# Copies of q and k through DRAM spread over two issuing queues from the first unit on, and four-term x sums at fixed places on VectorE

## The chip, the core and the metric

The kernel runs on one NeuronCore of a Trainium2 chip. The core has a matrix engine (TensorE, PE in the profile), a vector engine (VectorE, DVE), a scalar engine (ScalarE, ACT), GpSimd (POOL) and a synchronising engine (SyncE, SP) that here does little but issue DMAs. Each engine runs its own instructions in order and waits on semaphores for the others. ScalarE too can issue DMAs; such an issue then stands in ScalarE's own instruction order, among its evictions. The page writes ACTq and SPq for what these engines' queues do beside computing. The metric is device time in microseconds.

## The reference, cut to what matters

```python
# lightning attention: q, k, v of (B 4, H 8, S 768, D 64), a decay lam for each head, blocks of 64
for b in range(nb):
    intra = einsum(einsum(qb, kb) * Dmask, vb)
    inter = einsum(qb * lam_pow, kv_state)
    out[:, :, sl] = intra + inter
    kv_state = lam_block * kv_state + einsum(kb * rev_pow, vb)
# bridge: (B,H,S,D) -> x of (3072, 512); then four experts
p = domain_probs / (domain_probs.sum(-1, keepdims=True) + 1e-09)
for e in range(4):
    h = maximum(x @ w1[e], 0)          # w1[e]: 512 x 1024
    out += p[:, e:e + 1] * (h @ w2[e]) # w2[e]: 1024 x 512
```

All of it is fp32.

## The kernel before

The 3072 tokens are cut into three groups of 1024. A **unit** is one expert on one group; there are twelve, in the order group 0 with experts 0, 1, 2, 3, group 1 with 1, 2, 3, 0, group 2 with 2, 3, 0, 1. Both products of an expert are done in Strassen's way: seven products M1 to M7 of half-size blocks in place of eight, each of sums of blocks of the weights and of x. Most of these seven are cut once more in the same manner. The sums of weights are made by GpSimd ahead of time, written to DRAM (`w_ops`, `w_sums`) and read again (`ws_in`, `w2t`); the sums of x (tile `xs`, one "slot tile" for each of the seven) are made in place, by GpSimd for group 1 and by VectorE for the second unit and for group 2.

**Opening part.** The first chunks of attention run mixed with the first product of the first unit, `direct_product` (L1482, matmuls at L1503), in the order `SEQ0` = M1, M2, M5, M6, M7, M3, M4; the loop for the last five is at L1617 to 1632. Each of these has four quarters, and `sums_then` names what else is put behind a quarter.

**Main loop** (L1661 to 1755). For each unit there are seven steps, and each step has eight slots x = 0 to 7. In the slots the second product of the unit at hand (`second_product` L1086, matmuls into banks `q` at L1101, gate-weighted accumulation on VectorE at L1115 and L1119) alternates with the first product of the next unit (`first_product` L1023, matmuls into banks `pg` at L1047, in the order `SEQ` = M1, M5, M6, M2, M7, M3, M4). A `pg` bank is emptied by a copy on ScalarE at L1055 where its target is fresh, else by an addition on VectorE (helper `tt`, L117), followed for some targets by a relu on ScalarE at L1059. There are two `pg` banks in turn. From the sixth unit on both products are cut twice.

**The order is written out by hand** (`manual_schedule`): every engine executes in the order in which the Python code calls it. A planner on the Python side decides when some of the calls come: `now` counts slots, `busy` estimates GpSimd's backlog, `moved` that of the DMA engines (`send`, L109), `asked` that of SyncE (each `send` without a named engine adds 0.27 slots), `filled` that of VectorE. `pump` (L202) is called in each slot and takes the next chore (preparing weights on GpSimd) when GpSimd is free and neither `moved` nor `asked` is too far ahead. `until` forces chores that are needed now. `take(own_sums)` lets VectorE do one waiting x sum.

**DMAs.** `send` issues on SyncE unless an engine is named. DMAs issued on SyncE and on ScalarE share a ring of completion semaphores, so that an issue on the one can wait for an earlier DMA of the other. SyncE issues the loads of the weights (`w1b`, `w2b`), the stores of their sums, and the loads that feed the products: `feed` (L945) for `ws_in`, `feed2` (L1071) for `w2t`.

**Copies through DRAM.** The last two of six chunks of the sequence (`SECOND` = 4 on) get q and k by way of a DRAM tile `across`, in which the rows lie as the attention of group 2 wants them. `bring_across` (L453) lists 128 pieces, for q and k, 4 × 4 blocks and 4 batches; a piece copies 32 KB from DRAM to DRAM in runs of 128 B. All name `nc.scalar` as the issuing engine. `trickle` (L463) issues the next piece. It is called once per quarter in the last two products of the opening part, then in each odd slot of the main loop, and from step 4 on in slot 4 as well. `load_more` (L481), when the first chunk of a batch b is to be loaded, first issues all pieces of batches up to b that are left, and then loads `qx` and `kx` from `across` (`load_across`).

**Sums of x for the second unit.** `own(m)` (L1471) is a chore for each m: it has GpSimd make the weight operands for product m of the second unit, lets `own_x(m)` (L1433) append four in-place x subtractions to `own_sums`, and marks the product as fed. Subtractions not taken from `own_sums` by the time that `first_product` starts product m are all issued there, in a block.

Of the kernel before, what the change touches and what calls it, by code (L numbers as in the profile page):

```python
# [21 lines left out]
def kernel(  # L22
# [30 lines left out]
    nc = tc.nc  # L53
# [55 lines left out]
    def send(out, in_, by=None):  # L109
        n = 4 * min(packet(out), packet(in_))  # L110
        moved[0] = max(moved[0], now[0]) + 4 * math.prod(out.shape) / n * (9 + n / 25) / 16 / 1714
        if by is None:
            asked[0] = max(asked[0], now[0]) + 0.27
        (by or nc.sync).dma_start(out=out, in_=in_)
# [336 lines left out]
    pieces = []  # L451

    def bring_across(b):  # L453
        for x, of in enumerate((q, k)):
            for y in range(4):
                for ac in range(NHP):
                    src = of[b, 4 * (y // 2) + ac, SECOND * C:, (y % 2) * 32:(y % 2 + 1) * 32]
                    to = across[x, y * 32:(y + 1) * 32, ac, b]
                    pieces.append((b, lambda to=to, src=src: send(
                        out=to, in_=src.rearrange("(t p) d -> p t d", p=32), by=nc.scalar,  # L460
                    )))

    def trickle(m=1):  # L463
        for _ in range(m):
            if pieces:
                pieces.pop(0)[1]()

    def comes_across(n):
        return where(n)[0] >= SECOND
# [472 lines left out]
    SEQ = ("M1", "M5", "M6", "M2", "M7", "M3", "M4")  # L942
# [490 lines left out]
    def own_x(m, g=0, wait=0):  # L1433

        steps = to_do[m] = []

        def sub(f):
            def step():
                steps.pop()
                f()  # L1440
                if not steps:
                    made.add(("x", g, m))

            steps.append(step)

        for f in x_steps(g, m, nc.vector):
            sub(f)
        own_sums.extend(after(wait, f) for f in steps)
# [22 lines left out]
    def own(m):  # L1471
        if m not in own_ops:
            own_weights(m)
        own_x(m)
        fed[0, 1, m] = own_ops[m]


# [56 lines left out]
    def x_sums(*halves):  # L1534

        all_added()

        for name, a, b in (("T1", "B12", "B11"), ("T2", "B22", "T1"), ("T3", "B22", "B12"), ("T4", "B21", "T2")):
            for i in range(2):
                if (name, i) not in halves:  # L1540
                    continue
                tt(nc.vector, *(x_now[x][:, :, i * 256:(i + 1) * 256] for x in (name, a, b)), ALU.subtract)
# [59 lines left out]
    def sum_own(name, a, b, op=ALU.subtract):  # L1602
# [2 lines left out]
    sums_then = {  # L1605
        ("M5", 0): (lambda: x_sums(("T2", 0), ("T2", 1)),), ("M6", 0): (lambda: x_sums(("T3", 0)),),
        ("M6", 1): (lambda: x_sums(("T3", 1)),), ("M6", 2): (lambda: x_sums(("T4", 0)),),
        ("M6", 3): (lambda: x_sums(("T4", 1)), gates),
    }
    w2_steps = prepare_w2(1)  # L1610
    chores.extend((
# [5 lines left out]
    for m in SEQ0[2:]:  # L1617
        if m == SEQ0[-1]:
            for _ in range(2):
                feed2(*fill2.pop(0))  # L1620
        work = direct_product(m, blocks, ("g1", "g3")) if m != "M5" else [m5[1], *m5[3:]]
        for x, f in enumerate(work):
            f()
            for y in sums_then.get((m, x), ()):
                y()
            rest()
            if x < len(work) - 1:
                now[0] += 1
                take(own_sums)
                pump(0.75)  # L1630
            if m in SEQ0[-2:]:
                trickle()

    start, w1_steps = now[0], prepare_w1(2)

# [25 lines left out]
    for at, (g, e) in enumerate(units):  # L1661
        if at == 0:
            chores.extend(prepare_w2(2) + prepare_w1(3) + prepare_w2(3))
            chores.extend(prepare_w2_ops(2, False) + prepare_w1(0))
            for x in (3, 0):
                chores.extend(prepare_w2_ops(x, True))
        ahead = units[at + 1] if at + 1 < len(units) else None
        nested, nests = at >= NEST, ahead and at + 1 >= NEST
        if at == NEST:
            until(("w1", 0, "M4"))  # L1670
            chores.extend(prepare_w2_ops(1, True))
            spare.append(True)
        if at == NEST - 1:
            forget()
            packed.append(True)
        blocks, banks = {}, {}
        for i in range(7):
            if fill2:
                feed2(*fill2.pop(0))
            if not nested:  # L1680
                later_operands(g, e, SEQ2[i])
            if nested or (nests and i == 6):
                for _ in range(2 if ahead else 16 if i == 0 else 4 if i > 1 else 0):
                    if fill3:
                        feed3(*fill3.pop(0))
            if nests and i == 2:
                nc.scalar.dma_start(
                    out=gate_bc, in_=gate_rows[ahead[0] - 1, :, ahead[1]].partition_broadcast(P),
                )
            if nested:  # L1690
                pair = (at * 7 + i) % 2 if ahead else i % 3
                b = nested_product(at, SEQ3[i], (("q01", "q02"), ("q11", "q12"), ("g1", "g3"))[pair])
                if i < 6 and (at, SEQ3[i + 1]) != PLAIN:
                    inner_sums(at, SEQ3[i + 1])
            else:
                b = second_product(g, e, SEQ2[i], banks)
            if nests and i == 6:
                inner_sums(at + 1, SEQ3[0], nested)
                if at + 1 == EARLY[0]:
                    inner_sums(*EARLY, True)  # L1700
            a = []
            if ahead:
                a = first_product(*ahead, SEQ[i], blocks, ("g1", "g3"))
            if nested and (at, SEQ3[i]) == END:
                b[6:6] = [lambda: (give("M4", 1, ("s0", "s1"), (1,)), turn_end(1, "q11"))]
                b[5:5] = [lambda: (give("M4", 0, ("s0", "s1"), (1,)), turn_end(0, "q12"))]
            if not ahead:
                order = [[], b[0:2], [], b[2:4], [], b[4:6], [], b[6:]]
            elif nested:
                order = [b[0:2], a[0:2], b[2:4], a[2:4], b[4:6], a[4:6], b[6:8], a[6:8]]  # L1710
            else:
                order = [b[0:1], a[0:2], b[1:2], a[2:4], b[2:3], a[4:6], b[3:5], a[6:8]]
            turned_back = list(after_last.get(SEQ3[i], ())) if nested and not ahead else []
            for x, part in enumerate(order):
                for f in part:
                    if f:
                        f()
                now[0] += 1
                if (at - 2 * E + 1, i, x) in first_steps:
                    first_steps.pop((at - 2 * E + 1, i, x))()  # L1720
                if joins:
                    joined()
                elif (ahead or x % 2 == 0 and x + i) and not (nests and i == 6 and x == 7):
                    if nested or nests:
                        rest()
                    else:
                        took = False
                        for of in (lately, background, own_sums):
                            if of and (not took or fits() or of is background and len(of) > 1):
                                take(of)  # L1730
                                took = True
                if nested or nests:
                    take(aside)
                    if own_sums and fits():
                        take(own_sums)
                if ending and fits():
                    end_first()
                if nested and ahead and x in (1, 3) and fill3:
                    feed3(*fill3.pop(0))
                if turned_back and x > 0:  # L1740
                    for y in turned_back.pop(0):
                        if SEQ3[i] == END[1]:
                            give(*y[:2], ("s0", "s1"), *y[2:])
                        else:
                            give_across(*y)
                if fill and at * 7 + i >= 6 and x in ((0, 1) if at * 7 + i < 13 else (1, 3, 5) if at * 7 + i == 13 else FEED[nested]):
                    feed(*fill.pop(0))
                while steps and (at * 7 + i) * 8 + x == steps[0][0]:
                    steps.pop(0)[1]()
                if x % 2 or x == 4 and at * 7 + i >= 4:  # L1750
                    trickle()
                for h in range(1, NG):
                    if x == 3 and 0 <= at * 7 + i - FILL[h] < 7:
                        x_fill(h, SEQ[at * 7 + i - FILL[h]])
                pump(PACE[g])
# [30 lines left out]
```

## Time and profile before

| what | value |
|---|---|
| median of 3 runs | 1173.06 us (1172.74 to 1176.7) |
| the profiled execution, its own time | 1178.2 us |
| span of the profiled execution | 1176.4 us |
| mean granted TensorE clock in it | 0.995 |
| PE busy | 1148.0 us, 98% |
| VectorE, GpSimd, ScalarE busy | 828.1, 796.5, 316.8 us |
| bytes moved by DMA | 269.20 MB, mean 229 GB/s |
| DMA queues' share of 16 engines | q1 71.3%, q10 3.9% |

q1 carries the DMAs that SyncE issued, q10 those of ScalarE. The critical chain by engine is PE 84%, DMA 5%, DVE 5%, POOL 2%, and 1% each for ACTq, SPq and others.

How to read it: busy shares say only which engine is nearest to full; where one is at 98%, what remains is found in its idle times, by what each waited for, and then in the rows of the timeline around the longest of them. A row of the timeline gives the start in microseconds from the start of the span, the duration, the engine, the line of the kernel, the operation, the tiles written and read, and the number of instructions taken together. A bracket at its end says how long the engine was idle before it and what released it. For a window, the row gives busy time and number of instructions of PE, PE's weight loads, DVE, ACT and POOL, then the granted TensorE clock, the mean busy share of the 16 DMA engines, and GB/s.

### The profile page before, as it was taken

How to read it: one execution, taken by the hardware profiler on the slowest of the kernel's cores; microseconds unless marked ns; L12 is line 12 of the kernel's file. 1: busy time of each engine (PE TensorE's matmuls, PEld its weight loads, DVE VectorE, ACT ScalarE, POOL GpSimd, SP SyncE). 2: the span in 40 equal slices, each digit the busy share in tenths (PEclk: the TensorE clock that was granted, in tenths of full speed). 3: DMA queues.
4: the chain of work that ended last, by engine and by line, in shares of the span. 5: the costliest groups of instructions: out<-in, count | busy, mean ns of one | idle time of the engine just before them, and what ended most of it. 6: DMA issues, size and time to landing. Idle time of an engine off the chain costs nothing.

```text
span 1176.4 us, 21932 instructions
## 1 busy us (share of the span) xinstructions
PE 1148.0 (98%) x8011; PEld 992.5 (84%) x8011; DVE 828.1 (70%) x1516; ACT 316.8 (27%) x638; POOL 796.5 (68%) x752
## 2 busy tenths in 40 slices
PE   8999999999999979999999999999999999999998
PEld 7788888888887868888888888788888888888887
DVE  4576886578487728855775577898876677777785
ACT  3321122112201210121243342242244342341231
POOL 2846318647751939546789698897798793793894
PEclk9999999999999989999999999999999999999999
DMA  8874567999999969979577767986577867657542
GB/s 188 221 241 132 170 187 232 295 285 301 279 280 286 288 187 299 307 241 309 189 240 227 255 189 222 327 268 211 175 253 229 254 193 207 185 179 206 157 188 72
DMA packets 309257, 269.20 MB, mean 229 GB/s; under 512 B 141536, under 2 KB 244128, under 8 KB 309152
## 3 DMA queue, kind: packets, MB, share of 16 engines
q1 hardware_dynamic: 260544, 259.20, 71.3%
q10 hardware_dynamic: 48608, 8.62, 3.9%
q8 instruction: 64, 1.05, 0.4%
q14 instruction: 41, 0.34, 0.1%
HBM read 194.83 MB, written 77.10 MB: 231 GB/s over the span
## 4 chain that ended last, share of the span: by engine, by line
PE 84%; DMA 5%; DVE 5%; POOL 2%; issue 1%; SPq 1%; ACTq 1%; ACT 1%; POOLq 0%; DVEq 0%
PE pg L1047 35%; PE pq L1400 21%; PE q L1101 18%; PE pM L1503 2%; DMA ws_in<-w_ops 2%; DVE m L117 2%; PE pc L1503 2%; DVE xs L117 1%; DVE sums L117 1%; PE sp L694 1%; PE sp L701 1%; PE op L748 1%; DMA decay<-gate_rows 1%; PE op L766 1%; PE qp L664 1%
## 5 line engine op out<-in xcount | busy, mean ns | idle before, releaser
L1047 PE MATMUL pg<-xs,ws_in 128*128 128x256 f32 x1960 | 475.2, 382 | 12.1 <-ACT m L1055 7.2
L1047 PEld LDWEIGHTS pg<-xs,ws_in 128*128 128x128 f32 x1960 | 369.2, 190 | 69.0 <-DVE m L117 11.2
L117 DVE TENSOR_TENSOR m<-pg,m 128x512 f32<-128x512 f32 x451 | 307.3, 687 | 133.0 <-PE pg L1047 113.9
L1101 PE MATMUL q<-w2t,m 128*128 128x256 f32 x1120 | 265.3, 380 | 0.5 <-DVE m L117 0.5
L1101 PEld LDWEIGHTS q<-w2t,m 128*128 128x128 f32 x1120 | 213.0, 190 | 30.3 <-DVE m L117 1.2
L117 POOL TENSOR_TENSOR m<-m,decay 128x512 f32<-128x512 f32 x112 | 141.5, 1284 | 82.1 <-ACT m L1059 72.6
L1400 PE MATMUL pq<-acc,w2t 128*128 128x256 f32 x688 | 169.6, 379 | 1.5 <-DMA w2t<-w_ops 1.3
L117 DVE TENSOR_TENSOR sums<-pq,sums 128x256 f32<-128x256 f32 x272 | 112.8, 420 | 69.4 <-PE pq L1400 60.7
L1400 PEld LDWEIGHTS pq<-acc,w2t 128*128 128x128 f32 x688 | 130.3, 190 | 20.4 <-DVE m L117 1.7
L1059 ACT ACTIVATE m<-m 128x512 f32<-128x512 f32 x132 | 82.8, 630 | 200.7 <-DVE m L117 174.2
L117 DVE TENSOR_TENSOR m<-m,m 128x512 f32<-128x512 f32 x112 | 97.3, 869 | 7.2 <-ACT m L1059 7.2
L1055 ACT COPY m<-pg 128x512 f32<-128x512 f32 x88 | 51.6, 586 | 157.8 <-PE pg L1047 132.2
L1119 DVE SCALAR_TENSOR_TENSOR acc<-q,gate,acc 128x256 f32<-128x256 f32 x108 | 51.8, 479 | 51.2 <-PE q L1101 50.8
L117 POOL TENSOR_TENSOR acc<-hT,hT 128x512 f32<-128x512 f32 x56 | 70.5, 1277 | 8.6 <-PE pq L1400 8.6
L117 POOL TENSOR_TENSOR acc<-hT,acc 128x512 f32<-128x512 f32 x56 | 71.5, 1276 | 4.6 <-PE pq L1400 0.9
L1400 PE MATMUL pq<-hT,w2t 128*128 128x256 f32 x288 | 74.0, 379 | 0.1
L979 ACT COPY up<-m 128x512 f32<-128x512 f32 x56 | 32.5, 588 | 127.6 <-DVE m L117 127.4
L117 POOL TENSOR_TENSOR w2o<-w2b 128x512 f32<-128x512 f32 x26 | 34.6, 1350 | 41.8 <-DMA w2b<-in_moe_w_dram 24.3
L1400 PEld LDWEIGHTS pq<-hT,w2t 128*128 128x128 f32 x288 | 54.6, 190 | 7.9 <-DVE sums L117 0.5
L899 ACT COPY hp<-m 128x512 f32<-128x512 f32 x84 | 48.4, 589 | 43.8 <-POOL m L117 22.2
L1400 PE MATMUL pq<-m,w2t 128*128 128x256 f32 x228 | 58.5, 380 | 0.1
L117 POOL TENSOR_TENSOR acc<-m,acc 128x512 f32<-128x512 f32 x38 | 48.4, 1274 | 5.3 <-DMA partial<-acc 2.5
(140 smaller groups left out, 1342.0 us busy)
## 6 DMA issues: line engine op xcount, KB each, us to landing
w2t<-w_ops SPq DMA_DIRECT2D x129, 256.0 KB, 3.8
ws_in<-w_ops SPq DMA_DIRECT2D x40, 512.0 KB, 5.3
ws_in<-w_ops SPq DMA_DIRECT2D x60, 256.0 KB, 3.6
ws_in<-w_ops SPq DMA_DIRECT2D x40, 384.0 KB, 3.9
w2b<-in_moe_w_dram SPq DMA_DIRECT2D x56, 256.0 KB, 4.9
w_ops<-ops SPq DMA_DIRECT2D x28, 512.0 KB, 4.8
w2t<-w_sums SPq DMA_DIRECT2D x40, 256.0 KB, 4.4
w_sums<-w2o SPq DMA_DIRECT2D x16, 512.0 KB, 4.8
```

What stands on the lines that cost most here:

```text
L117: eng.tensor_tensor(out=o, in0=a, in1=b, op=op)
L664: nc.tensor.transpose(out=x[:, ac * C:(ac + 1) * C], in_=y[:, 2 * ac:2 * ac + 2].rearrange("p r d -> p (r d)"), identity=ident[:],)
L694: nc.tensor.matmul(out=sp[r][half[x], ac * BL:(ac + 1) * BL], lhsT=hc(kT)[half[r], ac, blk[x]], rhs=hc(qT)[half[r], ac, blk[x]], start=(ac ...
L899: nc.scalar.copy(out=there[x][:], in_=blk[at][:])
L979: nc.scalar.copy(out=there[at][:], in_=a[at][:])
L1047: nc.tensor.matmul(out=p[:, j * 256:(j + 1) * 256], lhsT=ws[i][:, j * P:(j + 1) * P], rhs=xs[i], start=(fresh and j == 0), stop=True, skip ...
L1055: nc.scalar.copy(out=new[at][:], in_=p[:])
L1059: nc.scalar.activation(out=new[at][:], in_=new[at][:], func=AF.Relu)
L1101: nc.tensor.matmul(out=p[:, s * DH:(s + 1) * DH], lhsT=h[A_OF[m]][:, c * 256 + s * P:c * 256 + (s + 1) * P], rhs=fed2[g, e, m][uu][:, c], ...
L1119: nc.vector.scalar_tensor_tensor(out=o, in0=x, scalar=w, in1=o, op0=ALU.mult, op1=ALU.add)
L1400: nc.tensor.matmul(out=p[:, 0:256], lhsT=fed3[e, m, x // 2][:, x % 2, c * P:(c + 1) * P], rhs=b[B_OF[i]][:, c * 256:(c + 1) * 256], start= ...
L1503: nc.tensor.matmul(out=p[:, s * 256:(s + 1) * 256], lhsT=a[c][:, f:f + P], rhs=b[:, c, j * 256:(j + 1) * 256], start=(s == 0 and c == 0 an ...
```

## The change

Two things change; no computation is added or left out.

The pieces of `across` are issued by SyncE or ScalarE. `trickle` gets the engine as an argument, with none meaning SyncE. It is now called after each quarter of the last five products of the opening part (SyncE), in every slot of the first unit (odd slots ScalarE, even slots SyncE), and in the odd slots of later units (SyncE). The additional call in slot 4 goes. Since `send` counts pieces without a named engine in `asked`, the planner sees 100 of the 128 there.

The x sums of the second unit are no longer appended to `own_sums` by the chore `own(m)`. Those for M1 are appended after quarter 1 of M3 in the opening part, those for the following six products at the start of steps 0 to 5 of the first unit.

```diff
-                    pieces.append((b, lambda to=to, src=src: send(
-                        out=to, in_=src.rearrange("(t p) d -> p t d", p=32), by=nc.scalar,
+                    pieces.append((b, lambda by, to=to, src=src: send(
+                        out=to, in_=src.rearrange("(t p) d -> p t d", p=32), by=by,
                     )))
 
-    def trickle(m=1):
+    def trickle(m=1, by=None):
         for _ in range(m):
             if pieces:
-                pieces.pop(0)[1]()
+                pieces.pop(0)[1](by)
...
     def own(m):
         if m not in own_ops:
             own_weights(m)
-        own_x(m)
         fed[0, 1, m] = own_ops[m]
...
-        ("M6", 3): (lambda: x_sums(("T4", 1)), gates),
+        ("M6", 3): (lambda: x_sums(("T4", 1)), gates), ("M3", 1): (lambda: own_x("M1"),),
     }
...
-            if m in SEQ0[-2:]:
-                trickle()
+            trickle()
...
+            if at == 0 and i < 6:
+                own_x(SEQ[i + 1])
             for x, part in enumerate(order):
...
-                if x % 2 or x == 4 and at * 7 + i >= 4:
-                    trickle()
+                if at == 0 or x % 2:
+                    trickle(1, nc.scalar if at == 0 and x % 2 else None)
```

## The prediction

> **What bounds the kernel now.** I read the busy shares first. TensorE (PE) is busy for 98% of the span, and no engine beside it comes near.
>
> ```profile
> span 1176.4 us, 21932 instructions
> ...
> PE 1148.0 (98%) x8011; PEld 992.5 (84%) x8011; DVE 828.1 (70%) x1516; ACT 316.8 (27%) x638; POOL 796.5 (68%) x752
> ```
>
> So a change that leaves the matmuls alone, as this one does, can win at most PE's idle time, 1176.4 − 1148.0 = 28.4 us, and what slow matmuls cost. Next I asked what ended PE's idle times: total, number, longest.
>
> ```profile
> PE pg L1047 <- ACT m L1055: 7.2, 1, 7.2
> PE pg L1047 <- DVE m L117: 5.8, 10, 1.4
> ...
> PE pg L1047 <- DVE xs L117: 1.4, 1, 1.4
> ```
>
> One stall of 7.2 us behind ScalarE (ACT) is a quarter of the idle time. The timeline around it (start, duration, and in brackets the idle time before it with its releaser) tells where it comes from.
>
> ```profile
> 412.51 11.04 ACTq L114 DMA_DIRECT2D across<-in_k_dram  x16
> 413.43 1.89 PE L1047 MATMUL pg<-xs,ws_in 128*128 128x256 f32 x8
> ...
> 423.59 0.59 ACT L1055 COPY m<-pg 128x512 f32<-128x512 f32 x1 [11.10 <-DMA across<-in_k_dram]
> ...
> 424.23 3.78 PE L1047 MATMUL pg<-xs,ws_in 128*128 128x256 f32 x8 [7.18 <-ACT m L1055]
> ...
> 427.80 2.25 PE L1101 MATMUL q<-w2t,m 128*128 128x256 f32 x8
> ```
>
> The reader sees ACT's instruction queue issue 16 copies in a row, 11.04 / 16 = 0.69 us each. The eviction at L1055 stands behind them in program order, so PE has no free bank. After the stall eight matmuls take 3.78 instead of 1.89 us and the next eight 2.25. The granted clock is 0.94 in the window 374 to 432, and 1.00 in those beside it.
>
> **Part 1: the copies leave ScalarE's burst.** There are 2 × 4 × 4 × 4 = 128 pieces. Before, ACT issues 10 in the last two products of the opening part, then four or five a step; at slot 170, where the first `load_across` must have batches up to 3, 16 are left and are forced. After, 23 go in five opening products, 56 in the first unit (28 on ACT, 28 on SyncE), 28 in the second and 21 in the third: 128 by about slot 154. Nothing is left at slot 170, and the burst goes. Gain: 7.18 us of idle, and (3.78 − 1.89) + (2.25 − 1.89) = 2.25 us of slow matmuls, together **9.4 us**. The clock agrees roughly: 0.06 × 58 = 3.5 us is the most that its window allows.
>
> On this point the Trainium skill, "TensorE: Matmul & The Clock Gate", section "What's actually happening", would price the clock's part a little lower: half speed after an idle window of about 3.4 us, until about 3.4 us of work have passed, costs an estimated 3.4 / 2 = 1.7 us, and the sum would be 8.9. The rows decide for me.
>
> ACT's other waits on these copies go with them: where a DMA issue stands in ACT's queue ahead of an evacuation and waits for an earlier DMA, PE pays through the sum on VectorE (DVE).
>
> ```profile
> 363.79 0.63 ACT L1059 ACTIVATE m<-m 128x512 f32<-128x512 f32 x1 [3.02 <-DMA w2b<-in_moe_w_dram]
> ...
> 367.24 1.99 PE L1047 MATMUL pg<-xs,ws_in 128*128 128x256 f32 x8 [1.43 <-DVE m L117]
> ...
> 394.34 0.63 ACT L1059 ACTIVATE m<-m 128x512 f32<-128x512 f32 x1 [3.50 <-DMA across<-in_q_dram]
> 394.36 1.99 PE L1047 MATMUL pg<-xs,ws_in 128*128 128x256 f32 x8 [1.32 <-DVE m L117]
> ```
>
> ACT has no other DMA there, so 1.43 + 1.32 and a following 0.25 at 371.21 go: **3.0 us**. Were the sums late for another reason as well, it would be 0.
>
> **What SyncE (SP) takes on.** It issues 100 pieces. One issue took 0.56 us on ACT's queue, and a comparable `qx<-across` 0.52 on SP's: 100 × 0.55 = 55 us of issuing, spread over some 340 us. From 240 to 400 us the issue records of SP, waits included, fill 12 to 17 us of each 20; the pieces were not on SP then. From 100 to 200 it is 5 to 13. In the second and third unit four pieces a step (about 15 us) add 2.2 us, so SP stands at 14 to 20 of 20: tight, not full, since part of those records is waiting. What is queued behind a piece are the `ws_in` and `w2t` loads; they wait for buffers that PE frees, are issued 6 to 14 slots of 1.9 us ahead, 11 to 26 us, and land after 3.6 to 7.4. A 0.55 us piece, or two, fits into the slack. Bounds: 0 if it always does; if 14 products (the second and third unit) are each late by 2 us, 28 us. I take 0.5, nearest to the row that the feeds show now: PE waited for a DMA of weights once, 1.3 us, in 1176.
>
> The 16 DMA engines carry the same bytes. By the DMA queues' rows, the ACT queue's share is 3.9% of 1176 us for 128 pieces and little else, so some 0.33 us for each on all sixteen. But the share by stage says when: 0.52 and 0.68 in 84–141 and 141–200, 0.94 to 0.98 in the three windows to 374, then 0.80 with the stall and 1.01 in 432–490.
>
> ```profile
> 84.00:141.00 57.00, 55.63 (x320) 48.52 (x319) 40.46 (x63) 9.39 (x16) 30.44 (x30) 1.00 0.52 155
> ...
> 374.00:432.00 58.00, 49.50 (x477) 41.66 (x476) 34.25 (x62) 10.82 (x23) 35.49 (x40) 0.94 0.80 223
> 432.00:490.00 58.00, 58.00 (x544) 50.09 (x544) 42.08 (x76) 7.78 (x21) 46.10 (x52) 1.00 1.01 307
> ```
>
> With the stall gone the loads of 432–490 are due 9 us sooner, when the rings are full. From 316 to 490 they were busy 0.98 × 58 + 0.80 × 58 + 1.01 × 58 = 162 us of 174; after, PE needs the same in 165. But some 30 pieces (48 before, 18 after) leave this stretch, 10 us: 152 of 165, which is 0.92. So I charge nothing; without that relief a few loads would be late, up to 3 us, the largest DMA wait that one weight load could explain.
>
> A rule that speaks against hoping for more: the skill's page "DMA: Bandwidth & Descriptors", section "Rules for kernel authors", says that spreading DMAs over issuing engines gives no bandwidth and saves only the sequencer's issue time. By it the turns of SyncE and ScalarE are worth nothing beyond ACT's freed issue slots.
>
> **Part 2: the x sums of the second unit.** `own(m)` no longer appends them; they are put in VectorE's order after a quarter of M3 (for M1) and at the start of each of six steps. The same sums, four of 128x256 for each product, about 1 us each; DVE's work does not change. For M1 the block of four stood ahead of the first evacuation, and PE's first product waited.
>
> ```profile
> 92.36 4.08 DVE L117 TENSOR_TENSOR xs<-xs 128x256 f32<-128x256 f32 x4
> ...
> 93.96 0.73 PEld L1047 LDWEIGHTS pg<-xs,ops 128*128 128x128 f32 x4 [1.75 <-POOL w2o L117]
> 93.99 1.10 PE L1047 MATMUL pg<-xs,ops 128*128 128x256 f32 x4 [1.37 <-DVE xs L117]
> ```
>
> The four now stand between evacuations of M3 and M4, some 10 us earlier, where DVE is little loaded (PE's matmuls set those products): **1.4 us** gained, 0 if the weights, which POOL released last, were as late as the sums. The blocks for M5, M6, M2, M7 move earlier within their steps and PE waited for none; 0. The block for M4 (178.34 to 181.89) stays, with its 1.06 us wait at 183.76.
>
> **What the moved pieces do to GpSimd (POOL).** DMA issues of SP and ACT wait in turn for an earlier one of either queue. Before, SP's `w2b` load at 81.99 took 5.16 us for two because ACT's pieces were before it, and POOL stood idle:
>
> ```profile
> 81.99 5.16 SPq L114 DMA_DIRECT2D w2b<-in_moe_w_dram  x2
> ...
> 85.57 2.51 POOL L117 TENSOR_TENSOR w2o<-w2b 128x512 f32<-128x512 f32 x2 [9.23 <-DMA w_sums<-w2o]
> ```
>
> That wait goes, but in the built order of the changed kernel a later half of the same matrix waits for a piece that ACT issues after the second eviction of the first unit (about 94 us). It lands near 98, the load near 103 (landing 4 to 5 us), POOL's 1.35 us follow, then 0.8 us of M5's operand: 104 to 106. PE needs that operand at 107.02 − 1.4 = 105.6. Cost 0 to 1, up to 3 if each landing is slow; I take **0.5**. Other POOL work is reordered by 1 to 14 slots, with the same forced places: −1 to +2, I take 0.4 lost.
>
> **Sum** on the profiled execution: 9.4 + 3.0 + 1.4 = 13.8 gained, 0.5 + 0.5 + 0.4 = 1.4 lost, net 12.4: span 1176.4 to 1164.0, its time 1178.2 to about 1166. The median of three runs, 1173.06, lies 5.1 us below the profiled one; part of that may be smaller stalls, so I take 12 off the median: **1161 us**.
>
> **Rivals.**
> A, partly given back (0.25): the wait on POOL at 105 costs its 3, and DMAs at full rings 3 more, or the 3.0 of ACT's waits return elsewhere. 13.8 − 8 = 6 off: 1167 (1164 to 1172). For it: the DMA share of 0.94 to 1.01. Against it: PE waited for weights once.
> B, slower (0.10): SyncE's queue, in order, becomes the bound. Pieces and buffer waits add until feeds of the second and third unit land after their product begins. It decides where the lead of about 11 us is used up by 4 to 7 of landing and 4 to 7 of queue: some eight pieces stuck in one row. Price 14 products × 1.5 to 2 = 21 to 28, less 13.8: 1180 to 1187. For it: 14 to 20 of 20 us. Against it: ACT's queue took 0.69 a piece even in the burst, and one piece per two slots (3.8 us) is no burst.
> C, the change does not reach the burst (0.03): 1172. The count, 23 + 56 + 28 + 21 = 128 by slot 154, is against it.
> The forecast itself has 0.62, with its own range of 1157 to 1164.
>
> **How the numbers follow.** The range of 1155 to 1174 holds the forecast, A and C; it leaves out B and a gain above 18. A measurement of this kernel can tell 0.5%, 5.9 us, from no change. Faster by more: 0.62 and half of A, 0.75; within: the other half of A and C, 0.15; slower: B, 0.10.
>
> **What would show it.** Right: no run of `across` on ACTq near 412, no L1055 wait of 11 us, granted clock 1.00 in 374–432, PE's first L1047 near 92.6 without a wait on `xs`, an SP queue with 100 pieces and no rise of PE's waits on `ws_in` and `w2t`. Wrong: PE waits on `ws_in`, `w2t` or `ops` above 2 us in all between 90 and 400 us, or POOL idle on `w2b` near 100 that PE then waits for. The sum is wrong also if the timed runs, unlike the profiled one, had a shorter burst.

## The result and the profile after

The changed kernel takes 0.9932 of the time of the kernel before (95% interval 0.9914 to 0.9951): 1166.03 us against 1174.51, medians of six runs each. Run again beside three experiments it was 0.9940 (0.9926 to 0.9954). So 7 to 8.5 us went, where 12 were forecast. The profiled execution has a span of 1167.8 us (1176.4 before), and its own time is 1169.61, the longest of its six.

The burst and its stall are gone, and the granted clock in their window is 1.00. First PE's waits by releaser (total, number, longest):

```profile
PE pg L1047 <- DVE m L117: 5.7, 8, 2.5
PE op L766 <- issue: 2.7, 2, 2.2
PE pM L1502 <- ACT m L1512: 2.0, 1, 2.0
PE pq L1400 <- DMA w2t<-w_ops: 1.4, 1, 1.4
```

then the windows (busy time of PE, its weight loads, DVE, ACT, POOL; clock, DMA share, GB/s):

```profile
84.00:141.00 57.00, 57.00 (x313) 50.03 (x315) 37.47 (x66) 10.19 (x17) 29.27 (x30) 1.00 0.56 163
...
374.00:432.00 58.00, 56.97 (x551) 48.87 (x546) 39.95 (x69) 14.02 (x31) 50.34 (x57) 1.00 0.95 288
432.00:490.00 58.00, 58.00 (x529) 50.09 (x528) 48.79 (x84) 7.79 (x18) 40.98 (x46) 1.00 0.89 274
```

The reader sees PE busy for 56.97 of 58 us where it was busy for 49.50, and no wait in 84 to 141, where the 1.37 us on `xs` stood. But two entries of the first list are new in size or place: a wait of 2.0 behind ScalarE at L1512 in the opening part, and one of 2.5 on VectorE. To find what they cost I compared the starts of the same work in both traces: the groups of attention matmuls at L748, which have the same place in PE's order, and the last `yp` matmul that waits (L1227).

| stretch of the program | before | after | difference |
|---|---|---|---|
| start to the L748 group at about 151 us | 150.71 | 151.08 | +0.4 |
| to the group at 361 | 210.29 | 210.55 | +0.3 |
| to the group at 441 (429 after) | 79.77 | 67.72 | −12.0 |
| to the group at 506 (495 after) | 65.55 | 65.55 | 0.0 |
| to the wait at L1227 near the end | 659.87 | 662.68 | +2.8 |

The third row is the forecast gain, nearly whole. The first should have been a gain of 0.9. The last was expected to be near zero, with at most the 0.4 us that the forecast put on GpSimd's reordered work. The experiments ask what these two rows are.

### The profile page after: what moved, and what is told of

Same layout as the page of the kernel before. It is cut to its first block, busy times and chain, and to the rows that moved or that the text cites. A ratio compares the mean times of both kernels' runs of the same rounds, so it can differ in the third digit from the quotient of the medians.

```text
span 1167.8 us, 21962 instructions
## 1 busy us (share of the span) xinstructions
PE 1148.6 (98%) x8011; PEld 993.3 (85%) x8011; DVE 824.5 (71%) x1516; ACT 317.1 (27%) x638; POOL 796.9 (68%) x752
## 4 chain that ended last, share of the span: by engine, by line
PE 85%; POOL 6%; DVE 4%; DMA 3%; issue 1%; SPq 1%; ACT 0%; ACTq 0%; POOLq 0%; DVEq 0%
PE pg L1047 35%; PE pq L1400 21%; PE q L1101 18%; POOL acc L117 3%; PE pM L1502 2%; DVE m L117 2%; PE pc L1502 2%; POOL m L117 2%; PE op L748 1%; PE sp L694 1%; DMA w2t<-w_ops 1%; PE op L766 1%; SPq L114 1%; PE sp L701 1%; DVE sums L117 1%
## 5 line engine op out<-in xcount | busy, mean ns | idle before, releaser
L117 POOL TENSOR_TENSOR xs<-xs 128x256 f32<-128x256 f32 x28 | 23.8, 849 | 42.5 <-DMA xs<-x_blocks 40.9
```

The costliest lines, as they stand in the source:

```text
L117: eng.tensor_tensor(out=o, in0=a, in1=b, op=op)
```

## The experiments

A note on reading: a kernel's ratio is against the kernel before on the same chip; 0.001 is 1.17 us. Stretches of single executions in the first row of the table scatter by 1.5 us and more, as the clock of the opening part does (last section).

### The two parts alone

The copies alone, with the old place of the x sums:

```diff
 def own(m):
+    own_x(m)
...
-        ("M6", 3): (lambda: x_sums(("T4", 1)), gates), ("M3", 1): (lambda: own_x("M1"),),
+        ("M6", 3): (lambda: x_sums(("T4", 1)), gates),
...
-            if at == 0 and i < 6:
-                own_x(SEQ[i + 1])
```

> The change without its second part: pieces as in the changed kernel, x sums of the second unit as before. The trace of the changed kernel puts 9.6 us of gain at the burst's place (408 to 440 us), 2.2 us at ScalarE's other waits (361 to 408), 1.4 us at the first L1047, and some loss in the opening part and behind 506 us. Theory 1 (the copies carry the gain): 7 us below the kernel before, 1.4 above the changed kernel, with PE's 1.4 us wait on xs back. Rival (the sums matter more than their one wait, by freeing VectorE in the first unit): 3 us or more above the changed kernel.

Measured: 0.9937 (0.9924 to 0.9949), 7.4 us below. PE waits 0.94 us on `xs` at 95.25, and the third stretch takes 67.72 us, as in the changed kernel. The sums alone are the reverse edit on the kernel before:

> The change without its first part: x sums at the fixed places, all pieces on ScalarE as before, burst included. Theory 1: 1.4 us below the kernel before, no PE wait on xs near 94 us, and the 7.2 us stall behind the burst of 16 still there. Rival (the sums matter more): 3 us or more below. If the weights' operand were as late as the sums: no difference.

Measured: 0.9988 (0.9977 to 0.9998), 1.4 us below; no wait on `xs`, and the stall stands.

```profile
419.44 3.78 PE L1047 MATMUL pg<-xs,ws_in 128*128 128x256 f32 x8 [6.69 <-ACT m L1055]
```

So the copies carry the gain, and the sums by themselves bring about what their one wait cost, with an interval of 0.2 to 2.7 us. What they add on top of the copies is not resolved: the 1.4 us expected between the copies alone and the changed kernel came out as 0.6 and −0.4 against its two measurements, inside the intervals. The two rivals, effects of 3 us or more, are out.

### How much of a burst PE can bear

The kernel before, with the pieces begun two products earlier; seven are forced at slot 170 instead of 16:

```diff
-            if m in SEQ0[-2:]:
+            if m in SEQ0[-4:]:
                 trickle()
```

> The kernel before with the opening part's pieces begun two products earlier, so that the forced burst has about 7 pieces and not 16; all on ScalarE, sums as before. Theory 1 (a burst costs what it exceeds PE's cover: ScalarE waited 11.1, PE 7.2, so 3.9 us are covered by the two banks): 7 x 0.69 = 4.8, less 3.9, 0.9 us of PE idle and no slow matmuls: 8 us below the kernel before. Rival (each piece costs its share): 9 of 16 parts of 9.4, 5.3 us below.

Measured: 0.9939 (0.9925 to 0.9953), 7.2 us below; 5.3 would be 0.9955, just outside. The timeline decides it. From the L748 group at 407.34 to that at 430.54 it is 23.20 us, where the kernel before takes 31.99: 8.8 less. And the rows show why:

```profile
410.46 4.96 ACTq L114 DMA_DIRECT2D across<-in_k_dram  x7
...
415.46 0.59 ACT L1055 COPY m<-pg 128x512 f32<-128x512 f32 x1 [4.42 <-DMA across<-in_k_dram]
...
416.10 1.99 PE L1047 MATMUL pg<-xs,ws_in 128*128 128x256 f32 x8 [0.50 <-ACT m L1055]
```

ScalarE waited 4.42 us and PE 0.50, a difference of 3.92. In the kernel before it was 11.10 and 7.18, again 3.92, and with the sums alone 10.61 and 6.69, 3.92 as well. That much is covered by the matmuls that PE had still to do before it needed the bank; by these three rows, pieces within it cost nothing and beyond it each costs its whole issue time of some 0.7 us. The cover is not a constant of the kernel: in the reversed run further below, where ScalarE comes late to the row, it is 15.37 − 12.21 = 3.16 us. The eight matmuls after a wait of 0.50 take 1.99 us, not 3.78: the slow ones belong to the long stall.

### Turns, or one queue

All pieces at the changed kernel's places, on ScalarE alone, and then on SyncE alone:

```diff
-    def trickle(m=1, by=None):
+    def trickle(m=1, by=nc.scalar):
...
-                    trickle(1, nc.scalar if at == 0 and x % 2 else None)
+                    trickle()
```

> The changed kernel with all 128 pieces issued by ScalarE, at the same places. Tells whether the early start or the turns with SyncE carry the gain. Theory 1 (only the burst mattered, and one or two issues between evictions fit into ScalarE's 73% idle time): 8 to 11 us below the kernel before; the new wait in the opening part, of ScalarE's load of the gates' probabilities on a SyncE load (6.6 us), may go too, since the ring of semaphores is dealt out otherwise. Rival (issues on ScalarE wait for SyncE's loads in the ring and hold evictions up all the way from 84 to 400 us): several PE waits of 1 to 1.5 us behind L1059 or L1055, 3 to 6 us less gain, 1169 to 1172.

Measured: 0.9917 (0.9903 to 0.9931), 9.8 us below. The rival's waits between 84 and 400 us do not appear: PE waits there for 1.06, 0.44 and 0.59 us, at the three places where the changed kernel has 1.07, 0.44 and 1.03. It comes out of the opening part 3.5 us earlier (147.56).

> The changed kernel with all 128 pieces on SyncE, none on ScalarE. Tells what the turns with ScalarE in the first unit are worth. Theory 1 (SyncE has room in the first unit, 5 to 13 of 20 us): within 1.5 us of the changed kernel. Rival (SyncE's queue in order becomes the bound there): feeds late, PE waits on DMAs of ws_in or w2t or on ops, 3 us or more above the changed kernel.

Measured: 0.9955 (0.9943 to 0.9967), 5.3 us below the kernel before and 1.8 behind the repeated run of the changed kernel, whose interval overlaps. PE's waits on DMAs of weights are as in the changed kernel (one, 1.43 us at 891.86), so the rival's mechanism is not seen; in the opening part it has the 6.2 us ring wait of the next section, with PE waits of 2.30 and 1.46 us. Where the rest of the 1.8 us goes, if it is one, stays open.

### The opening part: a wait that only changed its place

In the changed kernel the load of the gates' probabilities, which ScalarE issues among its evictions, waits in the ring of semaphores for another DMA than before. The timeline of the changed kernel:

```profile
45.22 0.70 SPq L114 DMA_DIRECT2D across<-in_q_dram  x1
...
45.97 2.88 SPq L114 DMA_DIRECT2D w2b<-in_moe_w_dram  x4
...
49.29 0.38 ACTq L1571 DMA_DIRECT2D decay<-in_moe_domain_probs_dram  x1
49.77 0.59 ACT L1512 COPY m<-pM 128x512 f32<-128x512 f32 x1 [6.61 <-DMA w2b<-in_moe_w_dram]
...
50.40 3.05 PE L1502 MATMUL pM<-xs,w1b 128*128 128x256 f32 x8 [2.02 <-ACT m L1512]
...
54.35 1.13 PE L748 MATMUL op<-qs,kv 64*64 64x64 f32 x32 [0.89 <-DVE kv L117]
```

A piece now stands ahead of SyncE's `w2b` loads, and by the times of the rows it is the first of these that the probabilities' load must wait for. ScalarE stands for 6.61 us, and PE for 2.02 and 0.89. I took the load out of ScalarE's order:

```diff
     def load_probs():
-        nc.scalar.dma_start(out=probs, in_=moe_domain_probs.rearrange("(t p) e -> p t e", p=P))
+        nc.sync.dma_start(out=probs, in_=moe_domain_probs.rearrange("(t p) e -> p t e", p=P))
```

> The changed kernel with the one load of the gates' probabilities issued by SyncE in place of ScalarE. In the changed kernel this load stood in ScalarE's order at 49.3 us behind a ring wait of 6.6 us on a SyncE load, an eviction behind it came late, PE was idle for 2.0 and 0.9 us, and a clock of 0.62 to 0.70 followed from 50 to 60 us. Theory 1 (that new wait is where part of the forecast gain went): ScalarE's wait goes, PE's two waits go, 3 us below the changed kernel, and up to 6 where the low clock went with them. Rival (the opening part is bound by something else, such as the loads of SyncE): another wait takes their place and the time is within 1 us.

Measured: 0.9943 (0.9929 to 0.9957), not faster than the changed kernel. My theory fell, and the rival held: ScalarE's wait and PE's two waits did go, and another came instead. On VectorE a block of gate arithmetic fills 67.86 to 75.4 us, the evictions stand behind it, and PE waits for them (in the changed kernel the block stands at 72.43 to 76.7, and PE does not wait behind it):

```profile
79.09 3.32 PE L1502 MATMUL pM<-xs,w1o 128*128 128x256 f32 x8 [2.26 <-DVE m L117]
```

Then the pieces were begun one product later, with M6:

```diff
-            trickle()
+            if m != "M5":
+                trickle()
```

> The changed kernel without the pieces in product M5 of the opening part: they begin with M6, four fewer there, made good later. Theory 1 (the pieces in M5 come ahead of the gates' load in the ring and turn its predecessor into a late load): the 6.6 us wait of ScalarE gets shorter or goes, 0 to 3 us below the changed kernel. Rival (PE's waits near 50 us have another cause): the same waits, same time.

Measured: 0.9924 (0.9912 to 0.9936), 0.9 and 1.9 us below the two measurements of the changed kernel, with intervals that overlap. ScalarE waits for no DMA there, and PE leaves the opening part at 148.34. The five executions with the pieces from M5 on SyncE and the changed planning (changed kernel 151.08 and 152.71, copies alone 151.98, probabilities on SyncE 150.48, all on SyncE 150.93) are all later than this one, and than those with ScalarE alone. But the first run of the next section has its pieces in M5 on SyncE too. There the same load is issued only at 48.78, PE waits 1.10 and 1.46 us at the two places, and it still leaves the opening part at 148.36, with a granted clock of 1.00 throughout. So the ring's wait alone does not explain the later end. Single executions do not size it, and the timed runs, one and two us with intervals that overlap, leave open whether it costs anything.

### Behind 506 us: the planner

`send` tells the planner how long the DMA engines will be busy (`moved`), and `pump` holds GpSimd's chores back by it. With the pieces at other places, chores come at other slots, in the whole first half. To undo that alone, the changed kernel's pieces are issued without telling the planner (neither `moved` nor `asked`), and a list of the same length feeds `moved` at the old places:

```diff
+    def plan(m=1):
+        for _ in range(min(m, len(planned))):
+            planned.pop(0)
+            moved[0] = max(moved[0], now[0]) + 4 * 8192 / 128 * (9 + 128 / 25) / 16 / 1714
...
+                if x % 2 or x == 4 and at * 7 + i >= 4:
+                    plan()
                 if at == 0 or x % 2:
                     trickle(1, nc.scalar if at == 0 and x % 2 else None)
```

> The changed kernel, but the planner's estimate of the DMA engines is fed as if the pieces were issued at the old places, so that GpSimd's chores come in the order of the kernel before. Theory 1 (the changed planning moved chores, and the 2.8 us lost behind 506 us come from it, a wait of 2.45 at 600 us among them): 2 to 3 us below the changed kernel, with PE's lead at 1140 us as large as at 506. Rival (the loss behind 506 us comes from the earlier time itself, loads that have less slack): within 1 us of the changed kernel, waits of the same size at the same places.

Measured: 0.9906 (0.9893 to 0.9918), 11.0 us below the kernel before, 3 to 4 below the changed one. The last stretch takes 658.37 us instead of 662.68. PE's waits from 432 to 1150 us, in the changed kernel

```profile
PE pg L1047 <- DVE m L117: 3.6, 6, 2.5
PE pq L1400 <- DMA w2t<-w_ops: 1.4, 1, 1.4
```

and in this one (its lines are 7 further on)

```profile
PE pg L1054 <- DVE m L117: 1.8, 6, 0.6
PE q L1108 <- DVE m L117: 0.5, 1, 0.5
```

The chain behind the wait of 2.45 can be read in the changed kernel's timeline:

```profile
571.41 0.92 SPq L114 DMA_DIRECT2D w2b<-in_moe_w_dram  x2
...
575.56 1.42 POOL L117 TENSOR_TENSOR ops<-w2b 128x256 f32<-128x256 f32 x2 [5.26 <-DMA w2b<-in_moe_w_dram]
...
581.02 9.20 POOL L117 TENSOR_TENSOR m<-m,decay 128x512 f32<-128x512 f32 x6
...
596.64 0.59 ACT L899 COPY hp<-m 128x512 f32<-128x512 f32 x1 [9.63 <-POOL m L117]
...
599.83 1.23 PE L1047 MATMUL pg<-xs,ws_in 128*128 128x256 f32 x4 [2.45 <-DVE m L117]
```

GpSimd is free at 570.30 for a chore whose load is issued only at 571.41, stands for 5.26 us, and then does the gating products `m<-m,decay` in one row from 581.02 to 590.2; the copies on ScalarE and the sums on VectorE follow late, and VectorE empties PE's bank late. With the old order there is no such wait for `w2b`, and the first of those products starts at 572.22, 5 us sooner when the 3.7 us are taken off by which that run is ahead at the 495 group. Behind the wait of 2.45 the granted clock falls, in this execution:

```profile
600.00:605.00 5.00, 5.00 (x16) 4.10 (x17) 3.85 (x7) 3.31 (x7) 4.48 (x4) 0.66 0.69 215
```

The 1.39 us at 893.76 has a like cause: six stores of weight sums stand in SyncE's queue between 883.87 and 887.39, ahead of the `w2t` load that PE needs. It is no clear loss, though, since the kernel before has such a wait at another place:

```profile
739.78 1.10 PE L1400 MATMUL pq<-acc,w2t 128*128 128x256 f32 x4 [1.30 <-DMA w2t<-w_ops]
```

So of the 2.8 us in the last row of the table 1.4 are idle time of PE (4.69 us in that stretch before, 6.07 after) and 1.4 slower matmuls (655.18 us of busy time before, 656.61 after).

The reverse, the kernel before with the changed order of chores:

> The reverse: the kernel before, with its pieces, its burst and its x sums, but the planner fed as if the pieces were at the changed kernel's places, so that GpSimd's chores come in the changed order. Theory 1 (the changed order of chores costs 2 to 3 us by itself): 2 to 3 us above the kernel before, PE waits of about 2.4 us near 608 and 1.4 near 903, and the stall of 7 us behind the burst. Rival (the loss behind 506 us comes with the earlier time, not the order): within 1 us of the kernel before.

Measured: 1.0042 (1.0029 to 1.0056), 5.0 us above, and more than expected. Its last stretch takes 661.20 us, 1.3 above the kernel before, with PE waits of 1.32 and 1.59 us at 612.80 and 905.69 and a wait of 5.6 us on `w2b` on GpSimd. The rest is the burst:

```profile
413.32 0.56 ACTq L459 DMA_DIRECT2D across<-in_q_dram  x1
...
413.92 10.71 ACTq L459 DMA_DIRECT2D across<-in_k_dram  x16
...
424.68 0.59 ACT L1062 COPY m<-pg 128x512 f32<-128x512 f32 x1 [15.37 <-DMA across<-in_k_dram]
...
425.31 3.78 PE L1054 MATMUL pg<-xs,ws_in 128*128 128x256 f32 x8 [12.21 <-ACT m L1062]
...
428.89 3.15 PE L1108 MATMUL q<-w2t,m 128*128 128x256 f32 x8
```

The piece ahead of the 16 stands in the kernel before too, at 411.91 while ScalarE's last copy still runs; here it is issued only at 413.32, some 4 us after ScalarE became free, so the stall grows from 7.18 to 12.21. The rows do not say why it came late. The whole stretch from 361 to 441 us takes 83.81 us here against 79.77. So the order costs 1 to 4 us behind 506 us, shown from both sides, but this run cannot size it alone.

### Together

> The changed kernel again, beside the three others on one chip. Every theory: 0.993 of the kernel before, 8 us below; PE waits of about 2.4 us near 600 and 1.4 us near 893.

Measured: 0.9940, as told above; PE waits of 1.32 near 600, where 2.4 was expected, and 1.14 near 893. The late products of GpSimd are there again (behind a wait of 5.17 us on `w2b`), but what PE pays for them differs between executions of one kernel.

> All 128 pieces on ScalarE at the changed kernel's places, and the planner fed as if they stood at the old places. Theory 1 (the two effects add: 9.8 us from the pieces on ScalarE alone, 2.5 to 3 from GpSimd's old order): 12 to 13 us below the kernel before, no PE wait above 1 us behind 500 us, and 2 to 4 us below the changed kernel. Rival (the old order of chores fits only the pieces on SyncE): no more than 10 us below the kernel before.

Measured: 0.9890 (0.9873 to 0.9906), 12.9 us below the kernel before and 5.9 below the changed one on the same chip (medians 1162.02, 1174.69, 1167.88), more than the 2 to 4 expected. Its last stretch takes 658.59 us.

> The changed kernel with both repairs: pieces from M6 on, and the planner fed with the old places. SyncE and ScalarE in turn as in the change. Theory 1 (effects add): 11 to 12 us below the kernel before, close to the run with all pieces on ScalarE and the same planning; the turns are then worth nothing. Rival (the turns matter): 2 us or more below that run.

Measured: 0.9900 (0.9886 to 0.9914), 11.7 us below. The turns of SyncE and ScalarE win nothing over ScalarE alone; the two intervals overlap, with ScalarE ahead by 1.0 us (1162.02 and 1163.04). These two also differ in where the pieces begin; with the same beginning and the old places planned it is 0.9890 with ScalarE alone against 0.9906 with the turns, on two chips.

The last stretch sorts the executions by the order of chores (the run with the half burst has a third order, and 659.49 us):

| order of GpSimd's chores | last stretch, us |
|---|---|
| old: before, sums alone, and the three with the old places planned (both queues, ScalarE, from M6) | 659.87, 659.82, 658.37, 658.59, 659.80 |
| changed: changed kernel (twice), copies alone, probabilities on SyncE, ScalarE alone, from M6, SyncE alone, old copies with new plan | 662.68, 661.30, 661.85, 662.49, 662.70, 661.33, 661.00, 661.20 |

The means are 659.3 and 661.8; the order costs **2.5 us** in this stretch. The records of GpSimd's instructions bear the grouping out: of some 745, the order differs at no more than 9 places between the changed kernel and the others of its group, and at no more than 7 between the kernel before and its group, some of them records that the traces lack, but at over 150 between the two kernels. The timed runs agree: telling the planner the old places is worth 3.1 to 4.0 us on the changed kernel, 3.2 with ScalarE alone and 2.8 with the pieces from M6, each pair measured on two chips.

## Why the forecast's steps held or failed

**The burst, 9.4 us: held.** From the L748 group at 408.78 to that at 440.77 it was 31.99 us; after, from 406.91 to 429.35, 22.44: 9.55 us less. The experiment with seven pieces shows the shape of the cost, nothing up to 3.9 us of cover and everything beyond. This term is the gain, and its mechanism is the one forecast.

**ScalarE's other waits, 3.0 us: the size nearly held, the cause is not shown.** The stretch ahead of that, from the group at 361 to the one at 409, shrank by 2.5, from 47.78 to 45.28. But it is 45.59 with the sums alone and 45.90 in the reversed run, where the copies stand on ScalarE as before, and 44.84 and 47.10 in the two kernels with all pieces on ScalarE at the new places. With the sums alone ScalarE still waits near 360,

```profile
359.86 0.63 ACT L1059 ACTIVATE m<-m 128x512 f32<-128x512 f32 x1 [3.23 <-DMA w2b<-in_moe_w_dram]
```

and PE does not wait behind it. So the 1.43 us at 367 went in kernels that kept the wait on ScalarE, and most of these 2.5 us may have come without the copies' leaving. Of the wait at 394 a part stayed, 1.03 us at 392.49 in the changed kernel: VectorE has transposes of `kx` and sums of its own ahead of that addition. The prediction named this, "late for another reason as well", and priced it at the whole.

**The issues on SyncE and the DMA engines, 0.5 us: held.** From 151 to 361 us, where SyncE has most of the pieces and the DMA engines are 69% busy up to 200 and 90 to 100% from there, it is +0.3, and −0.2 in the second execution. In the window 432 to 490 the DMA share fell from 1.01 to 0.89, near the forecast 0.92; the last piece is issued at 377.5. The rival B, SyncE's queue as the bound, is out.

**The x sums, 1.4 us: held,** 1.4 (0.2 to 2.7) by the timed runs of the sums alone, and the wait on `xs` is gone from the trace.

**The wait of GpSimd near 105 us, 0.5: seen, and covered.** It came where it was placed:

```profile
85.58 12.58 SPq L114 DMA_DIRECT2D w2b<-in_moe_w_dram  x2
...
100.91 1.27 POOL L117 TENSOR_TENSOR w2o<-w2b,w2o 128x512 f32<-128x512 f32 x1 [7.46 <-DMA w2b<-in_moe_w_dram]
```

The operand was ready by 105.3 and PE wanted it at 107.38, without a wait.

**"Other POOL work is reordered ... −1 to +2, I take 0.4 lost": this term failed in size.** It costs 2.5 us. The reordering was known from the built order; that it falls just where the kernel passes into the units with both products cut twice, with GpSimd on PE's path, was not followed up. The forced places were the same, but GpSimd comes to a chore before its load is even issued (570.30 and 571.41), and the gating products behind that chore come late.

**The opening part was not priced.** The forecast had one gain there (1.4) and one loss (0.5). The pieces from M5 on shift the ring of semaphores, ScalarE stands for 6.6 us (6.8 in the repeat), and PE is idle for 2.0 and 0.9 us (2.7 and 2.0), against which other waits of the opening part shrink. That ScalarE waits is shown; what the wait is worth is not, because taking it away put a wait of 2.26 in its place, and with the old places planned the opening part ends 2.7 us sooner with PE's two waits still there. Low clocks account for some of it: the changed kernel lost 3.4 us that way in its opening part, the run with the old places nothing.

Together: 9.55 + 2.5 gained in the middle, −0.3 in 151 to 361, −0.4 in the opening part with its gain of 1.4 included, −2.8 at the end, 8.6 on the profiled execution. The forecast was 12.4. Its own range was 1157 to 1164; the measured 1166.03 lies in that of the rival A, 1164 to 1172. Of the distance to 1161, 1.45 us come from the median before, which is 1174.51 by six runs and was 1173.06 by three. The rival A had the size, a gain partly given back, but neither of its two priced waits, at 105 us and at DMA engines that are full, is what took it: the order of the chores did, with an opening part that did not get shorter.

On the clock, the Trainium skill, "TensorE: Matmul & The Clock Gate", section "What's actually happening", has half speed for a while after an idle window. The rows agree in kind: the eight matmuls after 7.18 and 12.21 us of idle took 3.78 us, twice 1.89, and those after 0.50 us took 1.99. The loss by the rows is 2.25 us after the shorter stall and (3.78 − 1.89) + (3.15 − 1.89) = 3.15 after the longer; the estimate of 1.7 from that page is low for both.

On the turns, the skill's page "DMA: Bandwidth & Descriptors", section "Rules for kernel authors", has it that spreading over issuing engines gives no bandwidth. No run here gains by it: on one chip 0.9890 with ScalarE alone, 0.9900 with both (their pieces begin one product apart). These are times, not bandwidths.

## What to carry to other kernels

Look for DMA issues that stand in a row on an engine that also empties PE's banks: here a row within PE's cover (3.9 us) cost nothing, what went beyond it everything, and spreading the issues on the same engine was enough. When an edit feeds a planner, compare the planned order of every other engine as well, and keep the planner's inputs fixed to see the edit's own effect: 2.5 us of the gain was given back by chores that the edit did not mean to touch. A wait that is removed in a stretch where several engines are nearly late, such as an opening part, has to be tried, not subtracted. And a wait that is missing after the edit is the edit's doing only if it stays in kernels without it: the one at 367 us did not.

## What the runs showed of the hardware

The clock of the opening part differs between executions of near-identical programs. The kernel before has 0.66 in 15 to 20 us, the changed kernel 0.62 and 0.70 in 50 to 60, the changed kernel with the old places planned 1.00 in all windows to 84. One window of 5 us at 0.66 is 1.7 us lost; the changed kernel lost 3.4 that way in the opening part of its profiled execution, and 1.7 at 600 to 605, while that execution lies 3.6 above the median of its runs (1169.61 against 1166.03). Windows of this kind follow idle times of PE of 1.6 to 2.7 us here, but not each time: the same 2.2 us wait at 14.7 to 15.0 stands in executions with and without a low clock behind it.

DMA issues of two queues that share a ring of completion semaphores couple the queues both ways: in the changed kernel SyncE needed 12.58 us for two loads because its queue waited for an `across` copy of ScalarE's (the longest such wait of SyncE in the first 200 us is 11.8 us), and ScalarE stood for 6.61 us on a load that SyncE issued only while ScalarE waited.
